# Attention and gated feed-forward on one core: v loads issued ahead of the identity, and the mask constant made from it by a scan on VectorE

## The chip, the cores and the metric

The kernel runs on one core of one Trainium2 chip. The metric is the device time of one execution in microseconds; a kernel's time is the median over its runs. Less is better.

## The reference

There are 8 batches of 8 heads with 576 positions and 64 channels a head. Each head does causal attention whose scores carry a decay that is built from s; the result, 4608 tokens of 512 channels, goes through an RMS normalisation and a gated feed-forward layer with 1536 hidden channels.

```python
scores = scale * np.matmul(q, k.transpose(0, 1, 3, 2))
causal = np.triu(np.ones((S, S), dtype=bool), k=1)
cum = np.cumsum(np.maximum(s, 0.0), axis=-1)
bias = -(cum[:, :, :, None] - cum[:, :, None, :])
scores = np.where(causal, -1000000000.0, scores + np.minimum(bias, 0.0))
attn = softmax(scores)                       # with 1e-09 added to the sum
x = np.matmul(attn, v)                       # heads side by side: [4608, 512]
xn = x / np.sqrt(np.mean(x * x, -1) + 1e-06) * rms_g
g, val = xn @ w_gate, xn @ w_val
out = (g * (1.0 / (1.0 + np.exp(-g))) * val) @ w_out
```

## The kernel before, in words

**Staging.** Attention of batch b runs beside the feed-forward of the tokens of earlier batches. The tokens are cut into 9 chunks of 512; the loop over chunks c emits, in this order, the feed-forward's first half of chunk c (`ffn1_group`: gate and value matmuls, tanh on ScalarE, two products on VectorE), the preparation of batch c + 1, the loads of batch c + 2, the second half of chunk c (`ffn2`) and the attention of batch c + 1. Batch 0 has nothing to run beside: its loads, transposes and attention are the start-up of the kernel, and they are what the change touches.

**Order.** Nothing is issued where it is written. `I`, `fill` and `mms` hand every operation to a planner (class `Plan`) with an engine, an estimated duration and a key (a due time). The planner finds what each operation depends on from the tiles it reads and writes, and builds every engine's queue from the keys and its own estimates: of the operations that could start, the one with the least key goes first. `R.order(a, b)` makes b start after a has started, `R.after(o, p)` makes o wait for p. PSUM banks (`psa` to `psh`) are also given out by the planner. Where the planner expects TensorE to wait in the first 24 us, it puts filler matmuls (`spin`, L862, which multiply the tile `still`) into the gap. So a changed estimate or key can move instructions on all engines, and all names of PSUM banks.

Since every operation passes through these helpers, the profile puts VectorE, ScalarE, GpSimd and SyncE work at L388 (the helper `I`), memsets at L396 (`fill`), TensorE transposes at L403 and other matmuls at L405 (both in `mms`). One tells them apart by the tiles.

**The start-up's steps**, by the names in the profile:

- GpSimd issues the loads that convert from fp32 to bf16. The first four are parts of k and q of batch 0 (`load_runs`): 4 of every 9 rows first (`part=0`, list `kqa`), the other 5 of 9 later (`part=1`, list `kqb`). Both go into one buffer that the profile calls `q_nat`, as `q_nat<-in_k_dram` and `q_nat<-in_q_dram`. Then come five v loads (`v0`, into `v_nata`), then the gate and value weights in three blocks each (`wg_sb`, `wv_sb`), then the k and q of batch 1. `R.order(*loads)` fixes that order: kqa, two of v0, kqb, three of v0, weights. Eight such loads may be in flight.
- Between kqa and v0, GpSimd makes two constants. `make_identity` (masks.py:197 and 199) clears `ident_bf` and writes the ones of the diagonal with an `affine_select`. L781 and L782 do the same kind of thing for `tri`, which is 0 where the key's position in a block of 128 is not after the query's and -30000 elsewhere.
- VectorE copies `ident_bf` to fp32 (`ident_F`), and computes the decay (`decay`): the positive part of `s_all`, its running sum with a `tensor_tensor_scan`, and `half`. ScalarE makes `w_row` from it by an exponential. TensorE transposes `w_row` with `ident_F` (five matmuls), and VectorE copies the result to `wT`. Then VectorE clears the unused ends of several tiles (`KT`, `vw`, `mhalf`, `nrm`).
- For each of four head pairs TensorE transposes k and q (L403, operands `ident_bf` and `q_nat`), VectorE copies k to `KTa` and ScalarE copies q to `QTa`. This is done first for part 0 and later for part 1.
- Scores of a unit (a head pair and a half of the queries) follow at L405 with `KTa` and `QTa`. In batch 0, `tri` is added to the scores of a diagonal block by a matmul with `ident_bf`. ScalarE takes the exponentials (`Ea` to `Eh`), TensorE multiplies them with `vwa`, v scaled by `wT` on VectorE, and VectorE divides by the sum into `x_blka`. The first half's units need part 0 alone, the second half's need both.
- `x_blka` is squared, scaled by a root that GpSimd takes (`ala`), transposed and scaled by g into `xnT`, from which the feed-forward reads.

SyncE issues the load of s and of g at the start; its queue has no other part in the start-up.

Of the kernel before, what the change touches and what calls it, by code (L numbers as in the profile page):

```python
# [270 lines left out]
def kernel(  # L271
# [12 lines left out]
    nc = tc.nc  # L284
    fp32 = mybir.dt.float32
# [3 lines left out]
    ALU = mybir.AluOpType  # L289
# [27 lines left out]
    pers = ctx.enter_context(tc.tile_pool(name="pers", bufs=1))  # L317
# [3 lines left out]

    ident_bf = pers.tile([128, 128], bf16, name="ident_bf")
    still = pers.tile([128, 256], bf16, name="still")
    tri = pers.tile([128, 128], bf16, name="tri")
    ident_F = pers.tile([128, 128], fp32, name="ident_F")
    ident_f = ident_F[0:64, 0:64]
# [5 lines left out]
    s_all = pers.tile([BH, S], fp32, name="s_all")  # L332
# [43 lines left out]
    R = Plan(banks)  # L376
# [3 lines left out]
    def real(a):  # L380
        return a.get(banks) if isinstance(a, View) else a

    def I(eng, method, us, key=None, kind=None, dma=0.0, lags=(1.2, 1.2), **kw):
        outs = [kw[n] for n in ("out", "accum_out") if n in kw]
        ins = [a for n, a in kw.items()
               if n not in ("out", "accum_out") and isinstance(a, (bass.AP, View))]
        f = getattr(ENG[eng], method)
        o = R.add(eng, us, lambda: f(**{n: real(a) for n, a in kw.items()}), outs, ins, key=key,  # L388
                  lat=LAT[eng], kind=kind, dma=dma,
                  name=outs[0].bank.name if isinstance(outs[0], View) else outs[0].name)  # L390
        o.lags = lags
        return o

    def fill(eng, ap, value, us, key=None):
        f = ENG[eng].memset
        return R.add(eng, us, lambda: f(ap, value), [ap], [], key=key, lat=LAT[eng], name=ap.name)  # L396

    def mms(us, items, key=None):
        def emit():
            for out, lhsT, rhs, st, sp, tr in items:  # L400
                out = real(out)
                if tr:
                    nc.tensor.matmul(out, lhsT=lhsT, rhs=rhs, is_transpose=True, start=st, stop=sp)  # L403
                else:
                    nc.tensor.matmul(out, lhsT=lhsT, rhs=rhs, start=st, stop=sp)  # L405
        o = R.add("pe", us, emit, [i[0] for i in items],
                  [i[1] for i in items] + [i[2] for i in items], key=key, lat=0.22,
                  name=items[0][0].bank.name)
        o.n_mm = len(items)
        return o  # L410
# [8 lines left out]
    def bank(group, cap):  # L419
        return View(Bank(group, group, cap))  # L420
# [4 lines left out]
    def lay(b, dt, pattern=None, n=None, **sizes):  # L425
        a = b if dt == fp32 else b.bitcast(dt)
        a = a[:, 0:n] if n else a
        return a.rearrange(pattern, **sizes) if pattern else a


    def load_runs(b, which, h0, h1, key, part=0):
        c0, c1 = PARTS[part] if b == 0 else (0, KC)
        p0 = KP * which
        us = ((1.5, 1.6)[part] * (h1 - h0) / 8) if b == 0 else 2.85 * (h1 - h0) / 8
        return I("pool", "dma_start", 0.7, key=key, dma=us, lags=(0.95, 1.1),
                 out=raw[b][part][p0 : p0 + KP, h0:h1, :, :].rearrange("p h c d -> p h (c d)"),
                 in_=(k, q)[which][b, h0:h1, KP * c0 : KP * c1, :].rearrange(
                     "h (p c) d -> p h (c d)", c=c1 - c0))

    def load_row(dst, src, b, sc, eng, key):  # L440
        n = 128 if sc < 4 else 64
        return I(eng, "dma_start", 0.88 if eng == "pool" else 0.45, key=key, dma=1.2 * n / 128,
                 lags=(1.2, 1.2 if b < NRUN else MARGIN + 1.2), out=dst[0:n, sc],
                 in_=src[b, :, sc * 128 : sc * 128 + n, :].rearrange("h p d -> p h d"))

    def load_rows(dst, src, b, eng, key):
        return [load_row(dst, src, b, sc, eng, key) for sc in range(NB)]
# [68 lines left out]
    def decay(key):  # L516
        I("dve", "tensor_scalar", 0.5, key=key, out=s_all, in0=s_all, scalar1=0.0, scalar2=None,
          op0=ALU.max)
        I("dve", "tensor_tensor_scan", 1.3, key=key, out=cum, data0=ones[:, 0:1].to_broadcast([BH, S]), data1=s_all, initial=0.0,
          op0=ALU.mult, op1=ALU.add)  # L520
        I("dve", "tensor_scalar", 0.1, key=key, out=half, in0=cum[:, S - 1 : S], scalar1=-0.5,
          scalar2=None, op0=ALU.mult)
        I("act", "activation", 0.7, key=key, kind="exp", out=w_row[:, 0:S], in_=cum, func=AF.Exp,
          bias=half, scale=1.0)
        tp = lay(bank("w", 1), fp32, "p (c b) -> p c b", n=NB * BH, c=NB)
        mms(0.6, [(tp[:, sc, :], w_row[:, sc * 128 : (sc + 1) * 128], ident_f, sc == 0,
                   sc == NB - 1, True) for sc in range(NB)], key=key)
        I("dve", "tensor_copy", 0.42, key=key, out=wT, in_=tp)
        return tp
# [210 lines left out]
    def ffn2(c, key, step):  # L740
# [24 lines left out]
    STEP = PER / 144  # L765


    I("sp", "dma_start", 0.5, key=-100, dma=0.5, out=s_all, in_=s.rearrange("b h s -> (b h) s"))
    I("sp", "dma_start", 0.5, key=-90, dma=0.1, out=g4,
      in_=moe_rms_g.rearrange("(cc p) -> cc p", p=128))  # L770
    fill("dve", still, 0.0, 0.1, key=-101)
# [2 lines left out]
    def ident(t, key):  # L774
        R.add("pool", 0.5, lambda: make_identity(nc, t), [t], [], key=key, lat=0.06).n_pool = 2

    kqa = [load_runs(0, w, h, h + 8, -100) for h in range(0, H, 8) for w in range(2)]
    ident(ident_bf, -99.5)
    kqb = [load_runs(0, w, h, h + 8, -92, part=1) for h in (0,) for w in range(2)]
    v0 = load_rows(v_nat[0], v, 0, "pool", -94)  # L780
    R.add("pool", 0.25, lambda: nc.gpsimd.memset(tri, 0.0), [tri], [], key=-99.3, lat=0.06)  # L781
    I("pool", "affine_select", 0.35, key=-99.3, out=tri, in_=tri, pattern=[[1, 128]],  # L782
      compare_op=ALU.is_ge, fill=-30000.0, base=0, channel_multiplier=-1)
    I("dve", "tensor_copy", 0.15, key=-93.7, out=ident_F, in_=ident_bf)
    wl = []
    for i, (lo, hi) in enumerate(zip(WL, WL[1:])):
# [1 line left out]
            wl.append(load_w(w, lo * 128, hi * 128, -93 + 0.1 * i))  # L788
    dec = len(R.ops)
    wP = decay(-95)  # L790
    fills = []
    for t in KT:
        fills.append(fill("dve", t[:, :, S : NB * 128], 0.0, 0.17, key=-90))
# [10 lines left out]
    o = mms(0.1, [(gp_[:, 0:CC], g4, ident_F[0:CC, 0:CC], True, True, True)], key=-75)  # L804
# [9 lines left out]
    for o in R.ops[n0:]:  # L814
# [7 lines left out]
           in_=moe_rms_g.unsqueeze(0).to_broadcast([128, DM]))  # L822
    for c in range(NCH):
# [4 lines left out]
        b = c + 1  # L828
# [14 lines left out]
        if b + 1 < B:  # L843
            n = b + 1
            K2 = K - 14 + LEAD
            for sc in range(NB):
                for dst, src in ((k_nat, k), (q_nat, q)):
                    o = load_row(dst, src, n, sc, "sp", K2 + sc)
# [186 lines left out]
```

## Time and profile before

| | us |
|---|---|
| median of 5 runs | 352.3 |
| lowest, highest | 350.79, 354.44 |
| the profiled execution, its own time | 353.57 |
| its span, first to last instruction | 351.9 |
| TensorE busy | 341.3 (97%) |
| VectorE busy | 254.8 (72%) |
| ScalarE busy | 228.4 (65%) |
| GpSimd busy | 126.7 (36%) |

The profile is one execution. Its page gives each engine's busy time, the span in 40 slices with the busy share of each in tenths, the DMA queues, the chain of work that ended last, and the costliest groups of instructions. The trace behind it can be asked for a timeline, for who waited for whom, and for busy times in any stretch. The span is 1.67 us shorter than the execution's own time. TensorE's granted clock is 0.992 of full speed on the mean.

In the page's lines `PE` is TensorE, `PEld` its weight loads, `DVE` VectorE, `ACT` ScalarE, `POOL` GpSimd and `SP` SyncE; an engine's name with a q is its instruction queue. All times in the trace count from the start of the span.

### The profile page before, as it was taken

The page shows a single profiled execution, that of the slowest core. Times are in us where ns is not written, and L with a number is a line of the kernel's source. Part 1 is how long each engine was busy: PE and PEld are TensorE (multiplying, and loading weights), DVE is VectorE, ACT ScalarE, POOL GpSimd, SP SyncE. Part 2 cuts the span into 40 slices and gives each one's busy share as a digit, 9 for nine tenths or more (in the row PEclk, how much of TensorE's full clock was granted, in tenths as well). Part 3 has the DMA queues.
Part 4 walks back from the last instruction along what each step waited for, and adds up shares of the span by engine and source line. Part 5 has one row for each costly group of instructions (what it writes and reads, how often), then busy time and mean ns, then how long its engine had stood idle before and what let it go on. Part 6 is the DMA issues. An engine that isn't in the chain of part 4 may idle for free.

```text
span 351.9 us, 8062 instructions
## 1 busy us (share of the span) xinstructions
PE 341.3 (97%) x3037; PEld 209.3 (59%) x3037; DVE 254.8 (72%) x497; ACT 228.4 (65%) x467; POOL 126.7 (36%) x201
## 2 busy tenths in 40 slices
PE   7799999999999999999999999999999999999994
PEld 5579775787479765886544554455455444444443
DVE  5778878698568994989499958995787657707730
ACT  3679999786767986857685768666787433223321
POOL 8844393501481349014921393129225100000000
PEclk9899999999999999999999999999999999999998
DMA  7999998997887895989766886776741130020002
GB/s 141 213 209 207 264 189 196 194 221 174 205 154 217 152 208 84 230 164 198 121 186 162 196 170 144 209 170 133 177 83 29 58 106 0 1 91 30 0 32 96
DMA packets 140550, 51.16 MB, mean 145 GB/s; under 512 B 127316, under 2 KB 135256, under 8 KB 140504
## 3 DMA queue, kind: packets, MB, share of 16 engines
q1 hardware_dynamic: 131832, 41.13, 51.6%
q0 software_dynamic: 8672, 9.44, 14.7%
q8 instruction: 26, 0.43, 0.5%
q14 instruction: 20, 0.16, 0.2%
HBM read 38.16 MB, written 9.44 MB: 135 GB/s over the span
## 4 chain that ended last, share of the span: by engine, by line
PE 92%; DMA 3%; POOL 1%; DVE 1%; issue 1%; SPq 0%; ACT 0%; POOLq 0%; DVEq 0%; ACTq 0%
PE psc L405 14%; PE psb L405 12%; PE psf L405 12%; PE psd L405 11%; PE psa L405 11%; PE psg L405 11%; PE pse L405 10%; PE psh L405 9%; DMA q_nat<-in_q_dram 2%; DMA xnT<-x_blka 1%; POOL q_nat L388 1%; POOL v_nata L388 1%; PE psa L403 0%; PE psb L862 0%; PE psf L403 0%
## 5 line engine op out<-in xcount | busy, mean ns | idle before, releaser
L405 PEld LDWEIGHTS <-wg_sb 128*128 128x128 bf16 x624 | 60.0, 98 | 33.1 <-issue 1.3
L405 PEld LDWEIGHTS <-wv_sb 128*128 128x128 bf16 x624 | 59.7, 98 | 32.8 <-issue 1.8
L405 PEld LDWEIGHTS <-Hs 128*128 128x128 bf16 x444 | 41.1, 98 | 42.0
L388 POOL TENSOR_SCALAR_AFFINE_SELECT Eb<-Eb 128x512 bf16<-128x512 bf16 x7 | 4.5, 637 | 79.4 <-ACT Eb L388 79.4
L405 PE MATMUL psc<-wout_sb,Hs 128*128 128x512 bf16 x96 | 23.7, 379 | 0.0
L405 PE MATMUL psf<-xnT,wg_sb 128*128 128x256 bf16 (+1 forms) x116 | 20.6, 313 | 0.0
L388 DVE SCALAR_TENSOR_TENSOR x_blkb<-x_blkb,alb,gB 128x512 bf16<-128x512 bf16 x15 | 12.7, 892 | 11.0 <-POOL alb L388 11.0
L388 POOL TENSOR_TENSOR vwb<-v_nata,wT 128x512 bf16<-128x512 f32 (+1 forms) x20 | 20.3, 1039 | 0.0
L388 ACT ACTIVATE sq_scr<-x_blkb 128x512 bf16<-128x512 bf16 x20 | 12.6, 632 | 9.9 <-DVE x_blkb L388 9.6
L405 PE MATMUL psb<-wout_sb,Hs 128*128 128x512 bf16 (+1 forms) x84 | 19.0, 364 | 0.0
L405 PE MATMUL psa<-xnT,wv_sb 128*128 128x256 bf16 (+1 forms) x108 | 18.6, 308 | 0.0
L405 PE MATMUL psg<-xnT,wv_sb 128*128 128x256 bf16 (+1 forms) x108 | 17.6, 300 | 0.0
L388 ACT ACTIVATE sq_scr<-x_blka 128x512 bf16<-128x512 bf16 x18 | 11.4, 631 | 9.6 <-DVE x_blka L388 9.3
L388 ACT ACTIVATE sq_scr<-q_bf 128x1024 bf16<-128x1024 bf16 (+1 forms) x18 | 16.5, 916 | 0.2
L405 PE MATMUL psd<-wout_sb,Hs 128*128 128x512 bf16 (+1 forms) x72 | 16.4, 361 | 0.0
L388 ACT ACTIVATE sq_scr<-k_bf 128x1024 bf16<-128x1024 bf16 (+1 forms) x18 | 16.3, 907 | 0.0
L388 DVE CAST k_bf<-k_nat 128x512 bf16<-128x512 f32 (+1 forms) x30 | 16.1, 537 | 0.0
L388 POOL TENSOR_TENSOR vwa<-v_nata,wT 128x512 bf16<-128x512 f32 (+1 forms) x15 | 15.4, 1050 | 1.3 <-DMA v_nata<-in_v_dram 1.3
L405 PE MATMUL psc<-xnT,wv_sb 128*128 128x256 bf16 (+1 forms) x84 | 15.5, 318 | 0.3 <-DVE u_sbc L388 0.3
L388 POOL TENSOR_SCALAR_AFFINE_SELECT Ef<-Ef 128x512 bf16<-128x512 bf16 (+1 forms) x14 | 7.0, 525 | 23.7 <-ACT Ef L388 23.7
L388 DVE CAST q_bf<-q_nat 128x512 bf16<-128x512 f32 (+1 forms) x30 | 15.5, 517 | 0.0
L405 PE MATMUL psb<-xnT,wg_sb 128*128 128x256 bf16 (+1 forms) x92 | 15.5, 305 | 0.0
(475 smaller groups left out, 873.7 us busy)
## 6 DMA issues: line engine op xcount, KB each, us to landing
v_nata<-in_v_dram SPq DMA_DIRECT2D x24, 256.0 KB, 4.2
k_nat<-in_k_dram SPq DMA_DIRECT2D x24, 256.0 KB, 3.2
q_nat<-in_q_dram SPq DMA_DIRECT2D x24, 256.0 KB, 3.6
out_dram<-osba SPq DMA_DIRECT2D x12, 256.0 KB, 2.3
out_dram<-osbb SPq DMA_DIRECT2D x12, 256.0 KB, 2.7
out_dram<-osbc SPq DMA_DIRECT2D x11, 256.0 KB, 2.5
v_nata<-in_v_dram POOLq DMA_DIRECT2D x8, 256.0 KB, 9.6
wout_sb<-in_moe_w_out_dram POOLq DMA_DIRECT2D x2, 768.0 KB, 15.9
```

The source lines that it names most:

```text
L388: o = R.add(eng, us, lambda: f(**{n: real(a) for n, a in kw.items()}), outs, ins, key=key, lat=LAT[eng], kind=kind, dma=dma, name=outs[0]. ...
L405: nc.tensor.matmul(out, lhsT=lhsT, rhs=rhs, start=st, stop=sp)
```

## The change

GpSimd no longer clears the identity and no longer makes `tri`. VectorE clears `ident_bf`, GpSimd writes the diagonal with its `affine_select` as before, and this select is ordered after the second v load's issue. `tri` is made on VectorE from the identity: a scan along each row with a multiplier of one (the new tile `one`) turns the diagonal's one into a row of zeros up to the diagonal and ones from it on; subtracting 1 and multiplying by 30000 gives -30000 before the diagonal and 0 from it on. Both steps are made to come after `half`. The planner's estimate of the delays of the load of s goes from 1.2 us to 0.8 us on each side.

```diff
+    one = pers.tile([128, 1], fp32, name="one")
...
-    I("sp", "dma_start", 0.5, key=-100, dma=0.5, out=s_all, in_=s.rearrange("b h s -> (b h) s"))
+    I("sp", "dma_start", 0.5, key=-100, dma=0.5, lags=(0.8, 0.8), out=s_all, in_=s.rearrange("b h s -> (b h) s"))
...
-    ident(ident_bf, -99.5)
     kqb = [load_runs(0, w, h, h + 8, -92, part=1) for h in (0,) for w in range(2)]
     v0 = load_rows(v_nat[0], v, 0, "pool", -94)
-    R.add("pool", 0.25, lambda: nc.gpsimd.memset(tri, 0.0), [tri], [], key=-99.3, lat=0.06)
-    I("pool", "affine_select", 0.35, key=-99.3, out=tri, in_=tri, pattern=[[1, 128]],
-      compare_op=ALU.is_ge, fill=-30000.0, base=0, channel_multiplier=-1)
+    fill("dve", ident_bf, 0.0, 0.1, key=-100)
+    fill("dve", one, 1.0, 0.06, key=-100)
+    o = I("pool", "affine_select", 0.35, key=-99.5, out=ident_bf, in_=ident_bf,
+          pattern=[[-1, 128]], compare_op=ALU.not_equal, fill=1.0, base=0, channel_multiplier=1)
+    R.order(v0[1], o)
     I("dve", "tensor_copy", 0.15, key=-93.7, out=ident_F, in_=ident_bf)
...
     wP = decay(-95)
+    n = len(R.ops)
+    I("dve", "tensor_tensor_scan", 0.35, key=-89, out=tri, data0=one.to_broadcast([128, 128]),
+      data1=ident_bf, initial=0.0, op0=ALU.mult, op1=ALU.add)
+    I("dve", "tensor_scalar", 0.15, key=-89, out=tri, in0=tri, scalar1=-1.0, scalar2=30000.0,
+      op0=ALU.add, op1=ALU.mult)
+    for o in R.ops[n:]:
+        R.after(o, R.ops[dec + 2])
```

The planner makes new queues from this. As built, they differ from the old ones only up to the first feed-forward matmuls:

- GpSimd: kqa, two v loads, the identity's select, kqb, three v loads, weights. It had kqa, identity (2), `tri` (2), two v loads, kqb, three v loads, weights. Further on, two small copies into `vwb` change places with weight loads.
- VectorE: two more memsets at the start; `ident_F` after the decay's running sum and ahead of `half`; the scan for `tri` after the last clearing, then `wT`, then the second step of `tri`, then the `KTa` copies. In part 1 the `KTa` copies of the first two head pairs come together ahead of the fourth unit's division and the squares, and the three late v products come together ahead of the scaling of `x_blka`.
- TensorE: 25 fillers at the start where there were 30, then the transposes of `w_row`, then k and q of part 0 (`w_row` stood after the first head pair); 5 fillers after the second head pair. In part 1, the 6 fillers ahead of the scores into `Ef` are gone and 7 stand ahead of those into `Eg`, after the last head pair's transposes. The two transposes of `x_blka` stand together ahead of the last scores. The first group of gate matmuls stands ahead of the last attention-value group. In all there is one filler less.
- ScalarE: one small copy into `vwa` comes earlier. SyncE: no difference.

## The prediction

> **What bounds the kernel now.** I read the page's busy slices first, then the chain of waits over the first 24 us (the order of the engines' instructions differs between the two kernels only there), then the timelines of ScalarE, VectorE and GpSimd and the DMA share by the microsecond in the same stretch. The page says where the span goes:
>
> ```profile
> PE   7799999999999999999999999999999999999994
> ...
> DMA  7999998997887895989766886776741130020002
> ...
> PE 92%; DMA 3%; POOL 1%; DVE 1%; issue 1%; SPq 0%; ACT 0%; POOLq 0%; DVEq 0%; ACTq 0%
> ```
>
> After the second slice TensorE never falls under nine tenths: the feed-forward matmuls begin at 24.06 us and run almost without a gap to the end. So only a start-up of about 24 us can be shortened, and whatever moves that 24.06 us moves the end by as much. The chain of waits shows what the start-up hangs on (start, length, what):
>
> ```profile
> 2.23 0.69 POOL q_nat L388
> 2.92 0.18 POOL ident_bf masks.py:197
> ...
> 3.21 0.29 POOL ident_bf masks.py:199
> 3.50 0.17 POOL tri L781
> ...
> 3.73 0.55 POOL tri L388
> 4.28 1.77 POOL v_nata L388 x2
> 6.05 0.67 POOL q_nat L388
> 6.71 7.42 DMA q_nat<-in_q_dram
> ...
> 16.86 1.40 PE psb L862 x6
> ```
>
> GpSimd issues k and q, makes identity and mask, issues two v loads, then the second parts of k and q; the second q load lands at 14.13 us and everything waits for it. The last line is six filler matmuls (`spin`) on the path: the next scores start only when they end.
>
> The timelines of ScalarE and VectorE (start, length, operation, and in brackets the idle time before it and what ended it):
>
> ```profile
> 4.16 1.35 DVE L388 TENSOR_TENSOR_SCAN s_all<-ones,s_all 64x576 f32<-64x576 f32 x1
> ...
> 17.80 0.44 ACT L388 ACTIVATE QTa<-psh 128x320 bf16<-128x320 bf16 x1
> 18.97 0.60 ACT L388 ACTIVATE Ef<-psb 128x512 bf16<-128x512 f32 x1 [0.73 <-PE psb L405]
> ```
>
> ScalarE runs nearly without a gap from 16.22 to 23.70 us (Ee to Eh); its largest hole is the 0.73 us before Ef, which waits for the scores behind the fillers. The windows (busy time of PE, PEld, DVE, ACT, POOL, then clock, DMA share, GB/s):
>
> ```profile
> 5.00:6.00 1.00, 1.00 (x12) 0.90 (x10) 0.94 (x4) 0.28 (x1) 1.00 (x2) 1.00 1.47 199
> 8.00:9.00 1.00, 1.00 (x56) 0.70 (x48) 1.00 (x3) 0.74 (x4) 1.00 (x2) 1.00 0.85 132
> 13.00:14.00 1.00, 0.00 (x0) 0.00 (x0) 0.05 (x1) 0.00 (x0) 0.62 (x2) 1.00 1.00 322
> 16.00:17.00 1.00, 1.00 (x28) 0.73 (x26) 0.89 (x4) 0.78 (x2) 1.00 (x3) 0.50 1.45 200
> ```
>
> The DMA engines have a dip at 8 us between two full stretches; TensorE stands still at 13 us, and from 15.02 to 18.43 us its granted clock is 0.50.
>
> [...] the mask's `affine_select` took 0.55 us beside VectorE's work on s_all, the identity's, of the same shape, 0.29 us with VectorE idle. [...]
>
> **The change, part by part.**
>
> GpSimd. Two memsets and the mask's select leave, and the two v issues move ahead of the identity's select. The v issues start at 2.92 instead of 4.28 us and end near 4.7 us. Without a block the select runs 0.3 us with about 0.05 us ahead of it, and the second k issue starts at 5.07 instead of 6.05 us, 0.98 us earlier. But the select now falls into the scan of s_all (4.16 to 5.51 us)[...]: I take it to wait until about 5.48 us and to end at 5.77 us. Then the second k starts only 0.28 us earlier, and the second q issue at 6.43 us. Everything that GpSimd issues later (three v loads, the gate and value weights) follows by the same amount; SP's queue keeps its order.
>
> When does the second q land? The load before it decides as well: the queue drains the first k and q until about 6.5 us either way. What can be won is the dip: DMA shares from 6 to 10 us are 1.27, 1.02, 0.85 and 1.12; against the 1.25 that the following microseconds hold, 0.76 us of share is missing, 0.76 / 1.25 = 0.6 us. With v queued 1.36 us earlier the dip should mostly close. I take 0.4 us (q at 13.73 us); bounds 0.2 us (the issue alone, blocked) and 0.98 us (the issue alone, unblocked).
>
> VectorE. The two memsets early on (0.17 us for one the size of `still`, 0.06 us for one like `ones`) fall into its 2.4 us idle before 3.54 us: nothing. The identity's fp32 copy (0.23 us) moves behind the scan and waits for the select: 5.80 to 6.03 us. So half ends near 6.2 instead of 5.68 us, w_row on ScalarE (0.77 us) near 7.0 instead of 6.49 us. The mask's scan: from 1.35 us for 576 columns and 0.12 us for 3 columns, 0.12 + 125 x 1.23/573 = 0.39 us; its tensor_scalar, from 0.45 us for 576 and 0.14 us for one, 0.21 us. These 0.6 us, the 0.5 us delay and w_row's PSUM copy (0.49 us), now ahead of the first KTa copy, put that copy at 8.6 instead of 7.51 us. VectorE then worked without a real hole until 13.04 us, 5.53 us in all, 0.49 us of it the wT copy that now stands ahead: 8.6 + 5.04 = 13.6 us. That is under the cover of the wait for q (13.73 us), with 0.1 us to spare; if q lands 0.98 us earlier, the cover is gone and some 0.5 us of that gain is lost.
>
> TensorE. The w_row transposes (0.46 us) go ahead of the first k and q transposes, at about 7.0 us, where TensorE waits for q until 7.16 us: 0.3 us at most, under the same cover. Five of the first 30 fillers move behind the second head pair's transposes: no cost. The six fillers of 16.86 us move: seven now stand before the scores into Eg, and the transposes for the last head pair come ahead of them. The scores into Ef then follow the third pair's transposes at once (their KTa copy, once behind the squares, now comes second on VectorE). ScalarE's hole of 0.73 us closes. Seven fillers at 0.11 us at full clock (0.21 us at half) are 0.8 to 1.5 us, while ScalarE has Ef, Ef and QTa to do, some 1.4 us: hidden, barely at half clock. I take the whole 0.73 us; bounds 0 (the fillers fall on the path in their new place) and 1.2 us (1.40 us of path less 0.2).
>
> Behind that: both transposes of x_blka now stand ahead of the last scores, and the first gate group ahead of the last attention-value group. x_blka is scaled on VectorE after three v products, which by my times is done about 0.7 us earlier than before, so no loss. Weights: the second value block landed at 24.05 us and is first used at 26.68 us, the third at 32.0 and 37.62 us: an advance of 1.2 us is covered.
>
> The sum: 0.4 + 0.73 = 1.1 us. The profiled execution took 353.57 us, its span 351.9 us with 1.67 us around it; it would become 352.5 us. It lies 1.27 us above the median of the runs, 352.3 us, from which I forecast 351.2 us.
>
> **The rivals.**
>
> A, the gain is hidden: GpSimd's select is blocked, VectorE's first half becomes the last thing to end instead of q, and the moved fillers only change place. For it: 0.1 us to spare, and a filler count set by a plan and not by the trace. Against it: the DMA dip closes on its own account. Time 352.3 us, 0 to 0.3 us gained.
>
> B, slower: the clock. With 25 instead of 30 fillers TensorE has nothing from about 5.7 to 7.0 us. [...] If the clock halves for the 3.41 us after 8.2 us, the first half's scores and transposes (2.5 us of matmul on the alternating path) stretch; with 1.5 us more against a cover of about 0.5 us, and without the gain of A, the end moves by +1.0 us: 353.3 us. It decides from where the first half ends 0.5 us after q's landing.
>
> C, more than forecast: no block by the scan, q 0.9 us earlier, [...] full clock in the second half (scores that took 0.39 us take 0.28 us, some 0.5 us in all): 0.9 + 0.73 + 0.5 = 2.1 us, 350.2 us.
>
> That the change does nothing is excluded: the instructions of four engines stand in another order.
>
> **How the numbers follow.** Forecast 0.5, A 0.2, B 0.15, C 0.15. The five runs of before spread from 350.79 to 354.44 us, so a median carries about 0.8 us of its own. The likeliest case alone is 351.2 us, 350.2 to 352.2 us; with B and C at its edges and that spread the range is 349.6 to 353.3 us. A change under 1%, 3.5 us, can't be told from none in this kernel, and every case lies inside it: within 1% 0.86; the rest is for what I have not seen, 0.07 on each side.
>
> **What would show it right or wrong.** Right: the second q transposes start near 13.7 us; the identity's select lasts about 1 us, its end with the scan's; no ScalarE hole over 0.3 us before Ef; the first gate matmul near 22.9 us; TensorE's gap at 13 us about 1 us shorter. Wrong: a half-clock stretch from 8 us; the second q landing at 14.1 us with the dip gone; a first gate matmul at 24 us; or a difference that arises after 25 us, where I expect none.

## The result, and the profile after

The changed kernel took 354.17 us (median of 42 runs, 352.88 to 356.43), beside 353.63 us for the kernel before in the same session (79 runs, 350.36 to 355.59). The ratio over all runs is 1.0028, with a 95% interval from 1.0015 to 1.0041 (the medians differ by 0.54 us, the means by 0.98 us): about 1.0 us slower, where 1.1 us of gain was forecast. The profiled execution took 354.1 us, its span 352.4 us.

The start-up went nearly as forecast in this execution. The first gate matmul began at 23.05 us (24.06 before), so 1.0 us was won there; the last matmul ended at 347.00 us (346.79 before). From the first gate matmul to the last matmul TensorE needed 323.95 us instead of 322.73, and the gain was spent. Part of that 1.0 us was most likely luck: the stretch of half clock that the kernel before had from 15.02 us is missing in this execution. The window from 16 to 17 us shows it (the clock is the third figure from the end; it was 0.50 before):

```profile
16.00:17.00 1.00, 0.96 (x26) 0.73 (x30) 0.82 (x3) 1.00 (x4) 0.74 (x1) 1.00 1.55 187
```

In a second profile of the changed kernel (`after_again`, below) half clock stood from 17.06 to 20.47 us and the first gate matmul at 24.08 us; in a second one of the kernel before it stood at 24.56 us. The page, busy slices and share of the chain:

```profile
PE   7889999999999999999999999999999999999993
...
DMA  7999999899999897999978996889841130020012
...
PE 79%; DMA 13%; POOL 3%; DVE 2%; issue 1%; ACT 0%; SPq 0%; DVEq 0%; POOLq 0%; ACTq 0%
```

The DMA row is fuller than before almost everywhere, not only at the start: in slices 4 to 30 most digits of 7 and 8 have become 8 and 9. The chain runs through different things as well. It no longer goes through the second q load (start, length, what):

```profile
4.80 0.79 POOL ident_bf L389
5.59 1.35 POOL q_nat L389 x2
6.94 8.94 DMA v_nata<-in_v_dram
15.87 0.28 issue
16.16 17.34 DMA wv_sb<-in_moe_w_val_dram
```

A v load lands 8.94 us after its issue began (the same load took 7.92 us before), and a weight load waits for it. The timeline of GpSimd shows why that counts (start, length, operation, and in brackets the idle time before it and what ended it):

```profile
16.16 0.74 POOL L389 DMA_DIRECT2D wv_sb<-in_moe_w_val_dram  x1 [1.44 <-DMA v_nata<-in_v_dram]
17.65 0.62 POOL L389 DMA_DIRECT2D k_nat<-in_k_dram  x1 [0.75 <-DMA v_nata<-in_v_dram]
...
19.21 0.19 POOL L389 TENSOR_SCALAR ala<-ssa 128x2 f32<-128x2 f32 x1
```

GpSimd works through its queue in the order built. In this trace its 13th load waited 0.44 us for the fifth to land (the second k), the 14th 0.51 us for the sixth (the second q), and the 15th, the third value block, 1.44 us for the seventh (the third v): each for the load eight ahead of it. So a late v load holds the issues behind it, and the root `ala` behind those: 19.21 us (18.00 before). VectorE in the same stretch, then ScalarE:

```profile
4.16 1.35 DVE L389 TENSOR_TENSOR_SCAN s_all<-ones,s_all 64x576 f32<-64x576 f32 x1
...
8.13 0.67 DVE L389 TENSOR_SCALAR tri<-tri 128x128 bf16<-128x128 bf16 x1
8.22 0.57 DVE L389 COPY KTa<-psb 128x256 bf16<-128x256 bf16 x1
...
20.25 0.70 DVE L389 TENSOR_SCALAR x_blka<-x_blka,ala 128x512 bf16<-128x512 bf16 x2 [0.65 <-POOL ala L389]
```

```profile
17.32 0.61 ACT L389 ACTIVATE Ef<-psb 128x512 bf16<-128x512 f32 x1
...
22.02 0.60 ACT L389 ACTIVATE Eh<-psa 128x512 bf16<-128x512 f32 x1 [1.19 <-PE psa L406]
```

The hole of 0.73 us before Ef is gone, and one of 1.19 us before Eh has come. The second q load landed about 0.4 us earlier: TensorE's first transpose of it stands at 13.74 us (14.18 before), after a gap of 0.90 instead of 1.66 us. Before, then after:

```profile
14.18 0.21 PE L403 MATMUL psa<-ident_bf,q_nat 64*64 64x64 bf16 x1 [1.66 <-DMA q_nat<-in_q_dram]
13.74 0.21 PE L404 MATMUL psd<-ident_bf,q_nat 64*64 64x64 bf16 x1 [0.90 <-DMA q_nat<-in_q_dram]
```

The windows after the start-up hold the difference that I had not looked for. They show the stretch from 24 to 347 us of before, then of after (busy time of PE, PEld, DVE, ACT, POOL, then clock, DMA share, GB/s):

```profile
24.00:347.00 323.00, 321.52 (x2684) 194.97 (x2680) 238.27 (x448) 214.15 (x435) 108.73 (x169) 1.00 0.65 144
```

```profile
24.00:347.00 323.00, 321.33 (x2681) 194.36 (x2679) 236.99 (x446) 213.85 (x434) 109.50 (x169) 1.00 0.75 144
```

The same 144 GB/s keep the DMA engines busy for 0.75 instead of 0.65 of the stretch. The page's queue lines and median times from issue to landing, before first and then after, say which transfers (packets, MB, share of 16 engines; then KB and us):

```profile
q1 hardware_dynamic: 131832, 41.13, 51.6%
...
v_nata<-in_v_dram SPq DMA_DIRECT2D x24, 256.0 KB, 4.2
```

```profile
q1 hardware_dynamic: 131832, 41.13, 60.1%
...
v_nata<-in_v_dram SPq DMA_DIRECT2D x24, 256.0 KB, 5.1
```

Packets and bytes are the same; a packet of the hardware queue took 0.516 x 351.9 us x 16 / 131832 = 22.0 ns before and 25.7 ns after. Nearly all of this is in the queue's 122112 packets of 256 bytes: 18.8 ns on the mean before, 22.5 ns after. Yet the change touches none of SyncE's loads of q, k and v. This is the observation that in the end explained the result. I saw it late: the first experiments were made without it.

### The profile page after: what moved, and what is told of

The parts are those of the page before. It is cut to its first block, busy times and chain, and to the rows that moved or that the text cites. A ratio compares the mean times of both kernels' runs of the same rounds, so it can differ in the third digit from the quotient of the medians.

```text
span 352.4 us, 8063 instructions
## 1 busy us (share of the span) xinstructions
PE 340.8 (97%) x3036; PEld 208.6 (59%) x3036; DVE 254.6 (72%) x501; ACT 228.4 (65%) x467; POOL 127.1 (36%) x198
## 3 DMA queue, kind: packets, MB, share of 16 engines
q1 hardware_dynamic: 131832, 41.13, 60.1%
## 4 chain that ended last, share of the span: by engine, by line
PE 79%; DMA 13%; POOL 3%; DVE 2%; issue 1%; ACT 0%; SPq 0%; DVEq 0%; POOLq 0%; ACTq 0%
PE psh L406 12%; PE psb L406 11%; PE psa L406 10%; PE psd L406 10%; PE psf L406 9%; PE psg L406 9%; PE psc L406 9%; PE pse L406 8%; DMA v_nata<-in_v_dram 6%; DMA wv_sb<-in_moe_w_val_dram 5%; DMA out_dram<-osba 1%; POOL vwb L389 1%; POOL q_nat L389 1%; DMA xnT<-x_blka 1%; DVE Hs L389 1%
## 5 line engine op out<-in xcount | busy, mean ns | idle before, releaser
L406 PE MATMUL psh<-wout_sb,Hs 128*128 128x512 bf16 x96 | 23.7, 379 | 0.0
L406 PE MATMUL psd<-xnT,wg_sb 128*128 128x256 bf16 (+1 forms) x116 | 20.6, 313 | 0.0
L406 PE MATMUL psf<-xnT,wv_sb 128*128 128x256 bf16 (+1 forms) x108 | 18.6, 308 | 0.0
L406 PE MATMUL psa<-wout_sb,Hs 128*128 128x512 bf16 (+1 forms) x72 | 16.4, 361 | 0.0
L406 PE MATMUL psh<-xnT,wv_sb 128*128 128x256 bf16 (+1 forms) x84 | 15.5, 318 | 0.3 <-DVE u_sbc L389 0.3
L389 DVE CAST q_bf<-q_nat 128x512 bf16<-128x512 f32 (+1 forms) x30 | 14.6, 488 | 0.6 <-DMA q_nat<-in_q_dram 0.6
```

## The experiments

In all of them a ratio is that of a kernel's runs to those of the kernel before in the same session, with its 95% interval.

### The order alone, the moved work alone

`lags_only` is the kernel before with the one hint that makes the planner choose the new order:

```diff
-    I("sp", "dma_start", 0.5, key=-100, dma=0.5, out=s_all, ...)
+    I("sp", "dma_start", 0.5, key=-100, dma=0.5, lags=(0.8, 0.8), out=s_all, ...)
```

> The kernel before with one number changed: the planner's estimate of the delays of the s load, 0.8 us for 1.2 us. No work moves between engines, but the queues of TensorE, VectorE and ScalarE come out almost as in the changed kernel. Theory R (the new order of the queues costs the time): about +1.0 us, ratio 1.003; the scores into Ef early, then a TensorE gap of about 1 us ahead of the x_blka transposes. Theory W (the moved work costs the time): ratio 1.000 or below it.

Measured: 0.9973 (0.9953 to 0.9994), and in a later session (`lags_again`) 1.0005 (0.9981 to 1.0028).

> The order's hint alone again, beside the others on one chip: 0.997 as before (0.995 to 0.999) under every theory; if it comes out at 1.000, the gain of the order was scatter and the costs of the parts are to be read against 1.000.

`held` has all of the moved work, and otherwise the old order on every engine:

```diff
+    order = [o for o in order if o not in (t0, t1, sel, idF)]
+    for o, p in ((sel, v0[1]), (idF, sel)):
+        order.insert(order.index(p) + 1, o)
...
+    then(third, clear)                     # VectorE's two memsets behind an early one
+    then(max(fills, key=order.index), mask)  # scan and tensor_scalar
```

> All of the moved work (v loads ahead of the identity's select, identity cleared and mask made on VectorE), with the order of the kernel before held on every engine otherwise. Theory R: ratio 0.998 to 1.000, the second q load landing about 0.4 us earlier. Theory W: ratio 1.003, and the late v loads land later than in the kernel before although they are issued earlier.

Measured: 1.0013 (0.9995 to 1.0032). The changed kernel again and the kernel before again, beside them:

> The changed kernel again, beside the two others on one chip. Both theories: ratio 1.003. It shows as well how far a second profile agrees with the first: if the late v loads again land near 16 us, their lateness belongs to the kernel; if they land before 15 us, it belonged to that execution.

> The kernel before against itself: ratio 1.000. Its interval is what the other comparisons can tell. Its profile is a second look at the kernel before: the second q load near 14.1 us and the first gate matmul near 24.1 us, if these times belong to the kernel.

Measured: 1.0028 (1.0011 to 1.0045) and 1.0004 (0.9979 to 1.0029). So the new order does not cost (its gain in the first session did not come again in the second), and the changed kernel, which adds the rest of the change to it, was 0.55% slower than it in the same session: the rest of the change costs. `held` lies between what the two theories gave it, and its interval holds 1, so it does not decide.

### Which part of the moved work

Three kernels, all with the new order: `vfirst_lags` has only the v loads ahead of the identity, `tri_dve_lags` only the mask on VectorE, `after_selfirst` all but the forced place of the select.

```diff
# vfirst_lags, from lags_only
-    ident(ident_bf, -99.5)
+    sel = ident(ident_bf, -99.5)
...
+    R.order(v0[1], sel)
...
+    R.order(v0[1], tm)          # tm is the memset of tri on GpSimd
# after_selfirst, from the changed kernel
-    R.order(v0[1], o)
```

`tri_dve_lags` takes from the diff of the change all but the lines on `ident_bf`; the new tile `one` is among them.

> Before with the new order's hint on the s load, and only one part of the change: GpSimd issues the first two v loads ahead of the identity; clear, select and mask stay on GpSimd (behind these two loads). Theory V (the early v loads make the later loads land late and hold GpSimd's queue): the whole cost of the change is here, 1.002 to 1.004 of before, the third weight issues or the second k issue wait for v loads, as in the changed kernel. Theory M (the work moved to VectorE costs): no cost here, 0.996 to 0.998, as the order alone.

> Before with the new order's hint, and only the other part: the mask is made on VectorE by the scan and a multiply; the identity stays on GpSimd, ahead of the v loads. The v loads issue about 0.6 us earlier than in before because the mask's memset and select are gone from ahead of them, but not ahead of the identity. Theory V: 0.996 to 0.998, no GpSimd issue waits for v. Theory M: 1.002 to 1.004. If both parts cost half, 1.000.

> The changed kernel without the forced order: the identity's select stands ahead of the two v loads, all the rest as in the change (clear and mask on VectorE, the new order). The select meets VectorE's scan of s or not as it falls. Theory V: 0.996 to 0.998, faster than both kernels. Theory M: 1.002 to 1.004, as the change. If the select then takes 0.8 us as well, the lock with the scan alone is not the cost.

Measured: `vfirst_lags` 0.9985 (0.9967 to 1.0004), `tri_dve_lags` 1.0030 (1.0007 to 1.0052), `after_selfirst` 1.0032 (1.0010 to 1.0053). Theory V, early v loads that hold the queue, fell. The numbers agreed with theory M, that instructions on VectorE cost. In `after_selfirst` the select met no scan and took 0.31 us, so its blocking is not the cost either. But M had no mechanism: TensorE lost the time long after the mask was made. In `after_selfirst`, TensorE's waits from 25 us on (what waited, for what: us, times, longest):

```profile
PE psb L406 <- DMA xnT<-x_blka: 1.6, 1, 1.6
PE pse L406 <- DMA xnT<-x_blkb: 0.6, 1, 0.6
```

The gate matmuls of two chunks stood waiting for transposes by DMA, from 175.5 and 213.4 us. The queue lines of all ten profiles taken until then fell into two groups: 51.6 to 53.4% for the hardware queue in every kernel without the tile `one`, 59.5 to 60.2% in every kernel with it, whatever its order. The tile holds 4 bytes a partition, takes 32, and was declared third of all. So it moves nearly every other tile by 32 bytes: the buffers into which q, k and v are loaded (`k_nat`, `q_nat`, `v_nata`) were allocated on multiples of 512 bytes and now stand 32 past one. `tri_dve_lags`, `after_selfirst` and `held`, which I had read as tests of VectorE's work, were tests of the tile's place as well.

### The tile's place

`one_end` is the changed kernel with the tile declared behind all the others; no instruction and no order differs, and no other tile moves against the kernel before except three tiny ones. `pad32` is the kernel before with 32 unused bytes where the change put its tile, `pad64` with 64, `pad32_mp` with 32 ahead of the working buffers alone, so that weights and `xnT` stay.

```diff
# one_end, from the changed kernel
-    one = pers.tile([128, 1], fp32, name="one")
...
     sq_scr = mp.tile([128, 2 * DM], bf16, name="sq_scr")
+    one = mp.tile([128, 1], fp32, name="one")
# pad32, from the kernel before
     still = pers.tile([128, 256], bf16, name="still")
+    gap = pers.tile([128, 8], fp32, name="gap")
```

> The changed kernel with its new 4-byte tile (the row of ones for the scan) allocated behind all other tiles instead of third, so that no other tile moves in SBUF; every instruction and its order are those of the change. Theory A (the tile, which takes 32 bytes of each partition, moves all later buffers from multiples of 64 bytes to 32 past one, and their DMAs run slower): the hardware queue's packets take 52 to 54% of the span's 16 engines as in before, instead of 60%; v loads land in 4.1 us instead of 5.0; time 0.995 to 0.999 of before. Theory M (the mask's and the clear's instructions on VectorE cost): 1.002 to 1.004, as the change, whatever the DMA share.

> The kernel before, every instruction the same in the same order, with an unused tile of 32 bytes a partition allocated where the change puts its tile of ones. Theory A: hardware queue 59 to 61%, v loads 5.0 us, time 1.002 to 1.005. Theory M: 52 to 53% and 1.000.

> The same with an unused tile of 64 bytes a partition, so that all later tiles move, but stay on multiples of 64 bytes. Theory A, if the multiple of 64 decides: 52 to 54% and 1.000. If any move from the old places decides (a larger multiple, such as the 256 and 512 on which some of the buffers stood): near 60% and 1.002 to 1.005. Theory M: 1.000.

> The kernel before with the unused 32 bytes allocated only ahead of the working buffers (q, k, v, their transposes, x_blk, H): the weights, xnT and the small constants stay where they were. Theory A: if the loads of q, k and v and their transposes carry the cost, 57 to 61% and 1.001 to 1.005; if the weights and xnT carry it, near 53% and 1.000.

Measured: `one_end` 0.9989 (0.9968 to 1.0010), `pad32` 1.0050 (1.0031 to 1.0069), `pad64` 1.0003 (0.9981 to 1.0025), `pad32_mp` 1.0051 (1.0029 to 1.0073). Without the move the changed kernel's cost is gone; with the move alone, and not one instruction of the change, the kernel before has it. Theory M fell. `pad64` came out as neither reading had it: the hardware queue as busy as with 32 bytes moved (59.0%), and no cost in time. The queue line and the window of `one_end`:

```profile
q1 hardware_dynamic: 131832, 41.13, 53.0%
```

```profile
24.00:347.00 323.00, 321.55 (x2690) 195.30 (x2686) 238.44 (x449) 214.95 (x435) 109.53 (x169) 1.00 0.66 144
```

And of `pad32` the queue line, TensorE's waits from 25 us on, and GpSimd's queue in the start-up, where the same waits for v as in the changed kernel stand, though v is issued in its old place:

```profile
q1 hardware_dynamic: 131832, 41.13, 61.2%
```

```profile
PE psb L406 <- DMA xnT<-x_blka: 1.7, 1, 1.7
PE psh L406 <- DMA xnT<-x_blkb: 0.6, 1, 0.6
```

```profile
16.27 0.74 POOL L389 DMA_DIRECT2D wv_sb<-in_moe_w_val_dram  x1 [0.96 <-DMA v_nata<-in_v_dram]
17.59 0.62 POOL L389 DMA_DIRECT2D k_nat<-in_k_dram  x1 [0.58 <-DMA v_nata<-in_v_dram]
```

### Which boundary, and which buffers

`pad128` and `pad256` have 128 and 256 unused bytes in the tile's place. `pad_kqv` moves only the three load buffers:

```diff
# pad_kqv, from the kernel before
+    gap = mp.tile([128, 8], fp32, name="gap")
     k_nat = mp.tile([128, NB, DM], fp32, name="k_nat")
...
+    gap2 = mp.tile([128, 120], fp32, name="gap2")
     k_bf = mp.tile([128, NB, DM], bf16, name="k_bf")
```

> The kernel before with 256 unused bytes a partition where the change puts its tile: k_nat, q_nat and v_nat, which stood on multiples of 512, then stand on odd multiples of 256, so that a row of 256 bytes (one head) still fills one 256-byte block. Theory A256 (a 256-byte row that straddles a boundary of 256 bytes costs more): hardware queue 52 to 54%, v loads 4.1 us, no v load holds the queue, time 0.998 to 1.002. If a multiple of 512 decides, or any move: 59 to 61% and slower.

> The same with 128 bytes: every row of 256 bytes straddles a boundary, half on each side. Theory A256: hardware queue 58 to 61%, v loads 4.8 to 5.4 us, time 1.000 to 1.005 (as with 64 bytes, where the share rose to 59% and the time did not show it). If a multiple of 128 is enough: 52 to 54% and 1.000.

> The kernel before with 32 unused bytes ahead of k_nat and 480 behind v_nat: only the three buffers into which q, k and v are loaded stand 32 past a multiple of 512; all later buffers keep their place within 512 bytes. Theory A256, with the loads as carriers: hardware queue 57 to 61% and 1.002 to 1.005. If the transposes and x_blk carry it: near 53% and 1.000.

> The changed kernel with its new tile behind all others, again: 0.9989 before, so 0.997 to 1.000 of the kernel before; below 0.998 the forecast of the on-record prediction, 0.997, would hold for the change without the move of the buffers.

| kernel | load buffers stand past a multiple of 256 by | hardware queue | ns a packet | ratio |
|---|---|---|---|---|
| before | 0 | 51.6% | 22.0 | 1 |
| `pad256` | 0 | 51.4% | 22.0 | 0.9996 (0.9979 to 1.0013) |
| `pad128` | 128 | 57.6% | 24.6 | 0.9998 (0.9971 to 1.0026) |
| `pad64` | 64 | 59.0% | 25.3 | 1.0003 (0.9981 to 1.0025) |
| `pad32` | 32 | 61.2% | 26.3 | 1.0050 (1.0031 to 1.0069) |
| `pad_kqv` | 32 (these alone) | 60.5% | 25.9 | 1.0037 (1.0014 to 1.0059) |

On a multiple of 256 the queue's packets took 22.0 to 22.7 ns in all ten profiles, off it 24.6 ns and more, and the three load buffers alone bring nearly all of that. The engines that read these buffers are not slower: VectorE's casts of `k_nat` had a median of 420 ns before and 422 ns in `pad_kqv`, GpSimd's products from `v_nata` (into `vwb`) 1038 and 1037 ns. A row of 64 fp32 channels is 256 bytes: where the buffer begins on a multiple of 256 it stays within one block of that size, elsewhere it straddles two. The runs agree with theory A256 for the packets: the boundary counts, 22.0 to 22.7 ns on it, 24.6 to 26.3 ns off it. Why it counts they do not show. Off it, 128 bytes past, which splits a row into halves, was the cheapest place (24.6 ns) and 32 past the dearest (25.4 to 26.3 ns).

`one_end_again` took 0.9984 (0.9965 to 1.0002).

The last two asked whether the transposes' buffers have a boundary too, and for the intended change's gain a third time (label `one_end_kt`, the same kernel as `one_end`):

```diff
# kt_256, from the kernel before
+    gap = mp.tile([128, 16], fp32, name="gap")
     KT = ring(2, [128, HP, NB * 128], bf16, "KT")
```

> The kernel before with 64 unused bytes ahead of KT: the load buffers stay on multiples of 512, and the transposed k and q, the exponentials and x_blk, which stood 192 past a multiple of 256, stand on multiples of 256. If the transposes' buffers have a place of their own that counts (which would explain why 64 bytes ahead of everything cost no time): hardware queue below 51%, time 0.996 to 0.999. If only the load buffers count: 51 to 53% and 1.000.

> The changed kernel with its new tile behind all others, a third time, now beside the kernel with the transposes' buffers moved, on one chip: 0.9989 and 0.9984 before, so 0.997 to 1.000; the three together should tell whether the change without the move is faster than the kernel before.

Measured: `kt_256` 1.0023 (0.9998 to 1.0049) with the hardware queue at 52.4%: no gain, so that is not why the 64 bytes cost no time. (`pad128` has a companion of this kind: it puts the weights and `xnT`, which stood 128 past a multiple of 256, on one. No run has that alone.) `one_end_kt` 0.9979 (0.9961 to 0.9997). The three runs of `one_end`, weighted by their intervals, give 0.9983 (0.9972 to 0.9994): 0.6 us faster than before. It is the version that beats both kernels, the changed one by 1.0028 / 0.9983 - 1 = 0.45%, 1.6 us. Which part of the change brings the 0.6 us is not shown: the order alone had 0.9973 and 1.0005, `vfirst_lags` 0.9985.

## Why the prediction was wrong

The forecast lay on the wrong side: 1.1 us faster, measured 1.0 us slower. Of this 2.1 us, 1.6 us is the tile's move and 0.5 us an over-sized gain. (The base was low as well: 79 runs of the kernel before have a median of 353.63 us, the five shown ahead 352.3 us.)

- **The step that failed: "a difference that arises after 25 us, where I expect none".** From the first gate to the last matmul TensorE needed 322.5 us on the mean of the ten profiles whose load buffers stand on a multiple of 256 (322.1 to 323.4), and 324.0 us on the mean of the eight where they stand 32 past one (322.6 to 326.0): 1.45 us. The first gate matmul itself came no later in the eight (24.0 us on the mean) than in the ten (24.4 us). Waits for `xnT` explain about 0.9 us of it on the mean (1.0 us a profile in the eight, 0.1 us in the ten), but they are uneven: 0.44 and 0.58 us in the two profiles of the changed kernel, with 0.43 us in the first of the kernel before, and 0.2 us in `pad_kqv`. The rest is in small waits, such as the 0.26 us for VectorE's `Hs` at 86.48 us of the changed kernel, and in gaps that the profile puts down to nothing. The working priced the memset of `one` ("nothing", rightly) and listed instructions, orders and landings; the place that the tile takes, the first line of the diff, was no term in it.
- **"Everything that GpSimd issues later follows by the same amount": failed in the changed kernel.** Its third value block was issued at 16.16 us (15.60 before), batch 1's k at 17.65 us (16.33). In `one_end` they stood at 15.82 and 16.73 us with no wait for v. So with the tile's move `ala` comes late in the start-up, as the 0.65 us wait above shows, and "no loss" for `x_blka` fell with it. That the first gate matmul comes later for it is not shown: it stood at 23.05 and 24.08 us in the two profiles of the changed kernel, from 23.31 to 24.27 us in the three of `one_end`.
- **The identity's select blocked by the scan: right.** It took 0.79 us and ended at 5.59 us, 0.08 us after the scan's 5.51 us; I had 5.77 us. In `held` and `one_end` it took 0.79 us too; in `vfirst_lags` it began at 5.01 us and ended at 5.59 us as well; where it stood before the scan it took 0.29 to 0.31 us. The runs show that the select waits for the scan; what makes it wait they do not show. The evidence from before, the mask's 0.55 us, was weak: that select ran from 3.73 to 4.28 us, so only its last 0.12 us lay beside the scan, which began at 4.16 us, and it did not wait for the scan's end at 5.51 us.
- **The second q's landing: right in the one execution, by luck as far as can be told.** 13.74 us for 13.73 forecast. But the same transpose stood at 14.69 us in the second profile of the changed kernel, at 14.18 and 14.82 us in two of the kernel before, at 14.85, 14.17 and 14.19 us in those of `one_end`, so a gain of 0.4 us is below the scatter of this landing.
- **The ScalarE hole: mis-sized.** I counted the whole 0.73 us. It closed before Ef, but in the changed kernel 1.19 us came up before Eh, and in `one_end` 0.69 us before Eg, 0.36 us before Eh and 1.33 us before Eg in its three profiles. The hole moved to the scores that now stand behind the seven fillers, so the term is between nothing and a part of 0.73 us. That the fillers would only change place is what rival A had said. This is where the over-sized half microsecond most likely lies; no run separates it from the landing.
- **VectorE's sum: right in total, not in its terms.** The mask's scan took 0.37 us for 0.39, its tensor_scalar 0.67 us for 0.21, but the copy behind it began 0.09 us after it did. The first KTa copy stood at 8.22 us for 8.6 (the terms named in the prediction add to 8.9 us when put end to end), the half ended at 13.65 us for 13.6.
- **Rival B, the half clock from 8 us: did not happen** in the changed kernel, whose clock stayed at 1.00 until 350 us. TensorE was busy for 0.26 us from 6 to 7 us there (0.49 us before). That such idle time brings a stretch of half clock is not shown. In `after_selfirst` and `tri_dve_lags` half-clock stretches from 9.3 and 7.8 us did occur, with the first gate matmul at 23.25 and 24.77 us, inside the scatter of the others (23.05 to 26.02 us). What did happen in the changed kernel's first profile is a part of rival C, which the forecast's sum left out: full clock in the second half, where the scores into Ee took 0.28 instead of 0.39 us.

Shown by the runs: the tile's move makes the hardware queue's packets slower and costs 1.6 to 1.8 us (1.3 us where the load buffers alone move); it needs nothing else of the change. Argued, not shown: that the slower packets are what costs the time, by way of transposes that come late for TensorE. Against it stand 64 and 128 bytes, with the hardware queue at 59.0 and 57.6% and no measurable time lost on the mean of the runs, and why that is so stays open. The landings point to where: the `xnT` transposes of `x_blkb` took a median of 2.6 us from issue to landing with 64 and 128 bytes as before, 3.0 to 3.4 us in the three kernels with 32. But it was 2.6 and 2.9 us in the two profiles of the changed kernel and 2.9 us in `kt_256`, so this is a pointer and no proof.

A second pointer lies in the clock that each run was granted on the mean. Mean time in us by that clock, with the number of runs (the kernel before from all five sessions of the experiments):

| granted clock | before | `pad128` | `pad64` | `pad32` |
|---|---|---|---|---|
| 0.991 and less | 354.6 (85) | 353.3 (1) | none | 355.9 (4) |
| 0.992 to 0.996 | 353.4 (163) | 353.6 (10) | 353.5 (7) | 355.0 (11) |
| 0.997 and more | 351.5 (43) | 353.4 (3) | 353.7 (7) | 354.3 (7) |

At the highest clock 64 and 128 bytes went with about 2 us more, in ten runs together, and half of the runs of `pad64` fell there, where one in seven of the kernel before did. So part of their "no cost" may be a cost that a higher clock made up for. Whether the higher clock follows from the move or is chance is not shown, and at the middle clock the difference between 32 bytes and the two others remains.

## What to carry to other kernels

In a kernel whose tiles are placed one behind the other, as here, a new tile is a change to every tile declared behind it. Before pricing instructions, see where the buffers of the DMAs stand with and without it, and put small tiles last: here a tile of 4 bytes a partition moved the load buffers by 32 and cost 1.6 us. And compare the DMA queue's share at equal bytes in the two profiles before dividing a change into parts: here one line of the page separated the kernels into two groups that no order or engine explained, and three experiments were read wrongly for want of it.

## What the runs showed of the hardware that was not expected

- The hardware queue's packets took 22.0 to 22.7 ns on the mean with the load buffers on multiples of 256 bytes (ten profiles), 24.6 ns at 128 past (one), 25.3 ns at 64 (one) and 25.4 to 26.3 ns at 32 (eight), with the same 131832 packets and 41.13 MB.
- In a kernel that TensorE bounds for 323 of its 352 us, with the DMA engines busy for 0.65 of that stretch, moving the load buffers to 32 past cost 1.3 to 1.8 us of time. The transfers were covered on the mean; single transposes with a due time were not, up to 1.7 us in one wait of `pad32`; that such waits are the whole of the cost is argued and not shown.
- The runs of the kernel before that were granted a clock of 0.997 or more on the mean took 351.5 us, those with 0.991 or less 354.6 us. Most of its scatter goes with the clock.
- A scatter of 0.6 us in where one load lands was seen between two executions of the same kernel (14.18 and 14.82 us), so a single profile of each kernel can't show a gain of 0.4 us in a landing.
